# Gate and value products of the last two chunks by blocks of 128, group by group for both chunks

## The chip, the cores and the metric

One core of a Trainium2 chip runs the program. The metric is the device time of one execution in microseconds. The engines are TensorE (PE; its weight loads are shown as PEld), VectorE (DVE), ScalarE (ACT), GpSimd (POOL) and SyncE (SP, whose queue issues nearly all DMAs). All arithmetic is float32.

## The reference

An attention block with a threshold feeds a gated feed-forward block. What matters for the change is the second one.

```python
# q, k, v: (8, 8, 576, 64)
thresh = max(scores) - tau           # scores below thresh are dropped
x = softmax of what is left @ v      # -> (4608 tokens, 512)
g = x @ w_gate                       # (512, 1536)
val = x @ w_val                      # (512, 1536)
out = (g * sigmoid(g) * val) @ w_out # (1536, 512)
```

## The kernel before, in words

**Chunks.** The 4608 tokens are handled in nine chunks of 512. Chunks 0 to 7 are the first 512 tokens of each of the eight batches; the 64 tokens left over in each batch make up the ninth chunk, number 8. While the scores and the attention of batch b run, the feed-forward work of the batch before runs between them. Behind the last scores there is nothing left to run beside: the products of chunks 7 and 8 stand alone. This part, from the line `tail[0] = True` (L2321) on, is called the tail here.

**Groups.** Gate and value columns are taken in six groups (`NF2`) of 256 columns each. A group is a product of a token block (two halves of 256 tokens, by two halves of the 512 inputs) with a weight block (value and gate columns, by the same two halves). It is done as seven products of 256 x 256 x 256 in place of eight, with sums of the operands ahead of them and sums of the results behind them. The seven are the methods `p1` to `p7` of `Group` (L1092), done in the order p1, p4 of the group before, p5, p2, p6, p3, p7 (`gates_and_values`, L2157). Each `mul` (L1104) is four matmuls of 128 x 256. Results add up in PSUM: p1 fills a bank `a`, ACT copies it to a bank `b`, p2 adds to `a`, and p6, p7 and p4 add to `b` one after the other; between them ACT reads what `b` holds so far, multiplied by 0.5. `finish` (L1159) makes the gate: tanh on ACT, (1 + tanh) x value on DVE, times the gate half on POOL, or on DVE in the tail.

**Products by blocks.** In the tail `NestedGroup` (L1282) does two of the seven products, p5 and p3, by blocks of 128 once more: seven matmuls of 128 x 128 per block product in place of eight, which needs sums of blocks of x (`deepen_x`, L1258, on DVE) and of the weights (made long before, and read with the group's other weights from `sums_hbm`). Their results lie in two banks as seven blocks and are folded to a 256 x 256 result, by `fold` (L1218) from SBUF or by `fold_banks` (L1228) from PSUM.

**Weights.** A group has nine parts of 256 KB in `sums_hbm`. From chunk 2 on `load_flow` (L1034) reads them, for each chunk anew, in two DMAs of 1280 and 1024 KB into one of two places, two groups ahead.

**Outputs.** The six groups of a chunk give the hidden values `hall`, and `Deep` (L1640) multiplies them by the summed `w_out`, again as seven products, five of them by blocks of 128 in the tail. `early` (L1665), `late` (L1672) and `inner_sums` (L1684) sum hidden values for it, on DVE in the tail. Its first product `p1` runs ahead of the last group's p4 (`gates_end`, L1808). In the tail the order is: groups of chunk 7, outputs of chunk 7, groups of chunk 8, outputs of chunk 8. The tokens of chunk 8 come back from `last_hbm`, and `token_sums` (L1057) makes their three sums.

**What sets the order.** The TensorE products are written out in program order. Everything for DVE, ACT, POOL and SP goes through `Plan` (L28): each job has a cost, a rank and its dependencies, and the plan decides with these, at the time of writing the program, in which order each engine's queue holds them. On the chip each queue is worked in that order, and an instruction that waits holds up all behind it in its queue.

**Banks.** PSUM has eight banks. In the tail all are free for gates and values (`more_banks`, L2325).

Of the kernel before, what the change touches and what calls it, by code (L numbers as in the profile page):

```python
# [10 lines left out]
F32 = mybir.dt.float32  # L11
# [133 lines left out]
def kernel(  # L145
# [90 lines left out]
    e_tail = whole[:, ZONE + KW:ZONE + KW + CW]  # L236
# [13 lines left out]
    sums_hbm = hbm.tile([NF2, P, GW], F32, name="sums_hbm")  # L250
    stream_hbm = hbm.tile([3, P, 3 * QW], F32, name="stream_hbm")
# [840 lines left out]
    class Group:  # L1092
# [66 lines left out]
        def finish(self, t, gb, gj, hold, mv):  # L1159
# [9 lines left out]
            tt, eng, took = (dve_tt, "DVE", 0.62) if tail[0] else (pool_tt, "POOL", 1.3)  # L1169
# [12 lines left out]
        def p7(self):  # L1182
# [4 lines left out]
            tt, eng, took = (dve_tt, "DVE", 0.62) if tail[0] else (pool_tt, "POOL", 1.3)  # L1187
# [14 lines left out]
    AT = {0: (0, 0), 1: (0, 1), 5: (0, 2), 2: (0, 3), 3: (1, 0), 4: (1, 1), 6: (1, 2)}  # L1202

    class Seven(Buf):
# [23 lines left out]
        def fold_banks(self, banks_, *deps):  # L1228

            y = self.place.rearrange("p (x q) -> p x q", q=P)  # L1230
            q0, q1 = (h.ap().rearrange("p (x q) -> p x q", q=P) for h in banks_)
            twice = lambda x: x.broadcast_to((P, 2, P))
            j = job("ACT", 0.28, lambda: nc.scalar.copy(y[:, 4:5], q0[:, 0:1]), *deps, rank=0)
            j = job("DVE", 0.42, dve_tt(y[:, 0:2], twice(y[:, 4:5]), q0[:, 1:3], ALU.add), j, rank=0)
            j = job("DVE", 0.42, dve_tt(y[:, 3:5], twice(y[:, 1:2]), q1[:, 1:3], ALU.add), j, rank=0)
            j = job("DVE", 0.29, dve_tt(y[:, 1], y[:, 3], q0[:, 3], ALU.add), j, rank=0)
            j = job("DVE", 0.42, dve_tt(y[:, 2:4], twice(y[:, 4:5]), q1[:, 0:2], ALU.add), j, rank=0)
            return j, self.place[:, 0:DM].rearrange("p (f n) -> p f n", n=TC)

# [14 lines left out]
    sevens = {False: (Seven(s_main), Seven(e_main)), True: (Seven(vall[:, 0:CW]), Seven(e_tail))}  # L1254
    flat_s = deque([Flat(sevens[False][0])])
    x_deep = {}

    def deepen_x(c, *deps):  # L1258

        if tail[0]:  # L1260
            if "t" not in x_deep:
                x_deep["t"] = [qkp.tile([P, S], F32, name=name) for name in ("qT", "kT")]
            q_, k_ = x_deep["t"]
            ts = q_[:, 0:2 * P], q_[:, 2 * P:4 * P], k_[:, 0:2 * P], k_[:, 2 * P:4 * P]
        else:
            ts = *(x_main[:, n * 2 * P:(n + 1) * 2 * P] for n in range(3)), tmp.rearrange("p a f n -> p (a f n)")[:, 4 * HW:4 * HW + 2 * P]
            deps = *deps, *s_bufs[0].jobs
# [14 lines left out]
    class NestedGroup(Group):  # L1282
# [20 lines left out]
        def p5(self):  # L1303
            self.take_b()
            self.es = [take("pe") for _ in range(2)]
            m = self.nested(0, True, *(d for h in self.es for d in h.deps))
            self.s, e = sevens[tail[0]]
            self.c5 = self.s.fill(self.es, m, 0)
            self.s5 = self.s.fold("DVE" if tail[0] or self.g not in FOLDS[0] else "POOL", 0 if tail[0] else 1, *self.c5)

        def p3(self):
            m = self.nested(1, False, *self.c5)
            e = sevens[tail[0]][1]
            u = self.u1_buf
            if tail[0]:
                old, e.jobs = e.jobs, []
                j, y = e.fold_banks(self.es, m, *old)
                for h, full in zip(self.es, (True, False)):
                    h.read_by(j)
                    h.done(full)  # L1320
                g1 = job("DVE", 0.62, lambda: nc.vector.scalar_tensor_tensor(out=u.ap, in0=y, scalar=0.5, in1=u.ap, op0=ALU.mult, op1=ALU.add),
                         j, self.u1, rank=0)
            else:
                js = e.fill(self.es, m, 0)
                for h, full in zip(self.es, (True, False)):
                    h.read_by(js[1 if full else 0])
                    h.done(full)
                j = e.fold("DVE" if self.g not in FOLDS[1] else "POOL", 0, *js)
                g1 = job("DVE", 0.62, dve_tt(u.ap, u.ap, e.ap, ALU.add), j, self.u1, rank=0)
            e.jobs = [g1]  # L1330
            self.finish(0, u, g1, self.a, self.m2)
# [306 lines left out]
    AHEAD = 3  # L1638

    class Deep:  # L1640


        def __init__(self, c, mark):
            self.c = c
            halves = [hall[:, t].rearrange("p g f n -> p (g f) n") for t in range(2)]
            self.a11, self.a12, self.a21, self.a22 = (halves[t][:, k * NF2:(k + 1) * NF2] for t in range(2) for k in range(2))
            self.in_tail = tail[0]
            self.s2, self.s3 = (flow[:, lo:lo + KW].rearrange("p (f n) -> p f n", n=TC) for lo in (GW, GW - KW))
            self.place = flow[:, 0:KW]
# [4 lines left out]
            if tail[0]:  # L1654
                self.steps = deque([self.p1, self.gates_end, self.p2, self.p7_alone, self.p5_flat, self.p6_alone, self.p3_flat, self.p4_alone])
                self.spaces = [pall[:, n * CW:(n + 1) * CW] for n in range(5)]
                if c == B:
                    self.steps = deque([self.p1, self.gates_end, self.p2, self.p7_alone, self.p5_end, self.p6_alone, self.p4_alone, self.p3_end])
# [6 lines left out]
        def early(self, mark):  # L1665
# [4 lines left out]
            self.inner_sums(6, self.s3, free_place if self.in_tail else middle, j3)  # L1670
# [8 lines left out]
        def sum(self, out, a, b, op, x, *deps, rank=2):  # L1679
            fs = slice(2 * x, 2 * x + 2)  # L1680
            tt, eng, took = (dve_tt, "DVE", 0.62) if tail[0] else (pool_tt, "POOL", 1.3)
# [708 lines left out]
```

## Time and profile before

| what | value |
|---|---|
| three runs | 1349.41 us median (1348.5 to 1352.29) |
| the profiled execution | 1349.87 us; its span 1348.0, so 1.87 around it |
| granted TensorE clock | 1.00 |
| PE busy | 1334.6 us, 99% |
| DVE, ACT, POOL busy | 1066.5, 895.7, 778.0 us |
| DMA | 202.11 MB, 150 GB/s over the span |
| last attention product ends | 1130.86 us from the start of the span |
| groups of chunk 7 | 1135.74 to 1204.58, and p4 from 1209.27 to 1211.00 |
| outputs of chunk 7 | from 1204.58, until 1240.11 |
| groups of chunk 8 | 1240.11 to 1308.95, and p4 from 1313.64 to 1315.37 |
| outputs of chunk 8 | from 1308.95, until 1344.50 |

The busy table gives for each engine the busy time, its share of the span and the number of instructions. A float32 product is recorded as two records of a matmul, so a plain product of four matmuls counts x8 and one of seven blocks x14. The chain of waits goes back from the last instruction: at each step to what released it, or to the instruction before on its engine. A stretch line gives the busy time of each engine in a window, the granted clock, the busy share of the DMA engines and what they moved. In a timeline the columns are start, duration, engine, line, operation, out<-in and shape; what stands in brackets is the engine's idle time ahead of it and what ended it. PSUM banks carry the names pa, pb, pe, px, py and sc there. The helper `dve_tt` records all DVE sums at L928, `pool_tt` all POOL sums at L925.

### The profile page before, as it was taken

How to read it: one execution, taken by the hardware profiler on the slowest of the kernel's cores; microseconds unless marked ns; L12 is line 12 of the kernel's file. 1: busy time of each engine (PE TensorE's matmuls, PEld its weight loads, DVE VectorE, ACT ScalarE, POOL GpSimd, SP SyncE). 2: the span in 40 equal slices, each digit the busy share in tenths (PEclk: the TensorE clock that was granted, in tenths of full speed). 3: DMA queues.
4: the chain of work that ended last, by engine and by line, in shares of the span. 5: the costliest groups of instructions: out<-in, count | busy, mean ns of one | idle time of the engine just before them, and what ended most of it. 6: DMA issues, size and time to landing. Idle time of an engine off the chain costs nothing.

```text
span 1348.0 us, 40299 instructions
## 1 busy us (share of the span) xinstructions
PE 1334.6 (99%) x15914; PEld 1118.9 (83%) x15914; DVE 1066.5 (79%) x2860; ACT 895.7 (66%) x2315; POOL 778.0 (58%) x870
## 2 busy tenths in 40 slices
PE   9999999999999999999999999999999999999998
PEld 7777777787888878888888888887888889999998
DVE  7888898888887777888788888888788876586686
ACT  6888777767756677787777777778677773330330
POOL 2677497565685659745994689566965594000000
PEclk9999999999999999999999999999999999999999
DMA  8753324356557543746264636562565518524621
GB/s 178 206 186 96 79 58 133 122 149 177 153 166 225 169 126 92 211 137 203 62 201 145 216 97 195 158 215 69 139 212 145 171 57 270 195 96 165 210 80 32
DMA packets 216140, 202.11 MB, mean 150 GB/s; under 512 B 166800, under 2 KB 184208, under 8 KB 205200
## 3 DMA queue, kind: packets, MB, share of 16 engines
q1 hardware_dynamic: 212032, 198.62, 50.0%
q8 instruction: 126, 2.06, 0.6%
q10 hardware_dynamic: 3920, 0.92, 0.3%
q14 instruction: 62, 0.51, 0.1%
HBM read 172.36 MB, written 27.13 MB: 148 GB/s over the span
## 4 chain that ended last, share of the span: by engine, by line
PE 93%; DVE 2%; DMA 2%; POOL 1%; ACT 1%; issue 1%; SPq 0%; ACTq 0%; DVEq 0%; POOLq 0%
PE pb L1109 19%; PE pa L1109 13%; PE px L1711 12%; PE sc L1989 10%; PE xa L2088 9%; PE pe L1109 6%; PE po L1416 6%; PE pe L1294 4%; PE py L1711 3%; PE pv L1341 2%; PE pg L1341 2%; PE sc L1294 2%; PE py L1720 2%; PE sc L483 1%; PE pv L600 1%; DMA wo<-in_moe_w_gate_dram 1%
## 5 line engine op out<-in xcount | busy, mean ns | idle before, releaser
L2037 DVE SCALAR_TENSOR_TENSOR pall<-sc,th,pall 128x288 f32<-128x288 f32 x504 | 244.3, 513 | 42.0 <-ACT pall L2035 22.6
L1109 PE MATMUL pb<-xall,big 128*128 128x256 f32 x1152 | 273.9, 381 | 0.0
L2035 ACT ACTIVATE pall<-sc,nm 128x288 f32<-128x288 f32 x504 | 232.8, 498 | 33.6 <-DVE pall L2037 33.5
L1109 PEld LDWEIGHTS pb<-xall,big 128*128 128x128 f32 x1152 | 214.9, 190 | 30.7 <-issue 2.7
L2066 DVE STREAM_TRANSPOSE pall<-pall 128x576 f32<-128x576 f32 x252 | 188.4, 764 | 23.6 <-ACT pall L2064 15.6
L2064 ACT ACTIVATE pall<-pall,ri 128x288 f32<-128x288 f32 x388 | 179.0, 527 | 28.4 <-DVE ri L2052 27.5
L1109 PE MATMUL pa<-xall,big 128*128 128x256 f32 x768 | 183.1, 381 | 0.0
L925 POOL TENSOR_TENSOR hall<-hall,tmp 128x512 f32<-128x512 f32 x80 | 102.2, 1280 | 106.5 <-DVE hall L1164 86.0
L1109 PEld LDWEIGHTS pa<-xall,big 128*128 128x128 f32 x768 | 143.2, 190 | 21.7 <-issue 2.5
L2010 DVE TENSOR_REDUCE mx<-sc 128x2 f32<-128x576 f32 x168 | 125.9, 750 | 43.4 <-PE sc L1989 42.8
L925 POOL TENSOR_TENSOR big<-big 128x128 f32<-128x128 f32 (+3 forms) x174 | 129.1, 750 | 44.1 <-ACT big L1216 22.3
L1989 PE MATMUL sc<-kT,qT 64*32 64x288 f32 (+1 forms) x5376 | 144.7, 345 | 1.0 <-DVE pall L2037 1.0
L1989 PEld LDWEIGHTS sc<-kT,qT 64*32 64x32 f32 x5376 | 95.1, 106 | 50.0 <-issue 9.3
L2088 PE MATMUL xa<-pall,vall 64*32 64x288 f32 x4032 | 128.8, 404 | 0.4 <-PE px L1711 0.4
L2088 PEld LDWEIGHTS xa<-pall,vall 64*32 64x32 f32 x4032 | 75.4, 107 | 46.1 <-issue 4.3
L2061 POOL TENSOR_SCALAR pall<-pall,ri 128x288 f32<-128x288 f32 x116 | 58.7, 518 | 71.8 <-DVE ri L2052 70.0
L1109 PE MATMUL pe<-xall,big 128*128 128x256 f32 x384 | 91.4, 381 | 0.0
L2046 ACT COPY sums<-sums 32x6 f32<-32x6 f32 x336 | 66.6, 198 | 30.2 <-DVE pall L2037 26.1
L1163 ACT ACTIVATE vall<-tmp 128x512 f32<-128x512 f32 x96 | 59.9, 627 | 36.8 <-POOL tmp L925 17.3
L1109 PEld LDWEIGHTS pe<-xall,big 128*128 128x128 f32 x384 | 72.4, 190 | 11.1 <-ACT pall L2064 1.1
L2012 DVE TENSOR_REDUCE mx<-sc 128x1 f32<-128x288 f32 x168 | 75.0, 446 | 0.0
L925 POOL TENSOR_TENSOR big<-hall 128x384 f32<-128x384 f32 (+2 forms) x69 | 65.2, 969 | 14.6 <-PE pa L1109 14.5
(290 smaller groups left out, 2629.5 us busy)
## 6 DMA issues: line engine op xcount, KB each, us to landing
big<-sums_hbm SPq DMA_DIRECT2D x42, 1280.0 KB, 6.7
big<-sums_hbm SPq DMA_DIRECT2D x42, 1024.0 KB, 6.9
vall<-in_v_dram SPq DMA_DIRECT2D x112, 144.0 KB, 3.6
sums_hbm<-big SPq DMA_DIRECT2D x36, 256.0 KB, 3.6
out_dram<-big SPq DMA_DIRECT2D x32, 256.0 KB, 3.0
qT<-in_q_dram SPq DMA_DIRECT2D x112, 72.0 KB, 4.0
kT<-in_k_dram SPq DMA_DIRECT2D x112, 72.0 KB, 3.1
wo<-in_moe_w_gate_dram SPq DMA_DIRECT2D x16, 384.0 KB, 3.7
```

The costliest lines, as they stand in the source:

```text
L925: return lambda: nc.gpsimd.tensor_tensor(out=out, in0=a, in1=b, op=op)
L1109: nc.tensor.matmul(ps[:, i], w[:, k_, i * P:(i + 1) * P], x[:, k_, :], start=first and i == k_ == 0, stop=True, skip_group_check=True)
L1294: nc.tensor.matmul(self.es[b_].ap()[:, at_ * P:(at_ + 1) * P], ws[n], xd[o][n], start=b_ not in begun, stop=True, skip_group_check=True)
L1416: nc.tensor.matmul(ps, h(f), w[:, f, :], start=(f == 0), stop=(f == NF2 - 1))
L1711: nc.tensor.matmul(ps, a[:, f, :], ws[n][:, f, :], start=bank_ not in begun, stop=True, skip_group_check=True)
L1989: nc.tensor.matmul(pss[h][(slice(g * G, (g + 1) * G), *part)], qT[hs, col:col + G], kT[hs, c * SH + keys[0]:c * SH + keys[1]], start=True, ...
L2010: rs.append(job("DVE", 0.72, lambda n=n, tile_=tile_: nc.vector.tensor_reduce(out=mx[:, n:n + 2, 0], in_=tile_[:, :, 0:SH], axis=AX.X, op= ...
L2035: ej = job("ACT", 0.42, lambda x=x, n=n: nc.scalar.activation(ps[x], scs[x], AF.Exp, bias=nm[:, n:n + 1]), ej, masks.get((h, u - 1)), rank=0)
L2037: masks[x] = job("DVE", 0.45, lambda x=x, n=n: nc.vector.scalar_tensor_tensor(out=ps[x], in0=scs[x], scalar=th[:, n:n + 1], in1=ps[x], op0 ...
L2064: scaled.append(job("ACT", 0.46, lambda x=x, n=n: nc.scalar.activation(x, x, AF.Copy, scale=ri[:, n:n + 1]), rj, rank=rank))
L2066: seg["turned"].append(job("DVE", 0.72, lambda both=both: nc.vector.transpose(out=both, in_=both), *scaled, rank=rank))
L2088: nc.tensor.matmul(holds[a].ap()[x * G:(x + 1) * G, 0:SH].rearrange("d (i q) -> d i q", q=G), vr[rs, h, j, ds], p[rs, h, :, j, :], start=( ...
```

## The change

**Order.** In the tail the groups of the two last chunks stand side by side: group 0 of chunk 7, group 0 of chunk 8, group 1 of chunk 7, and so on, then the outputs of chunk 7, then those of chunk 8. A group is now a `Whole`, with the same seven products in the same order as before, all seven by blocks of 128.

**Banks.** The eight banks are four pairs; `a`, `b` and `e` are a pair each. All copies between them and all reads move 512 and 384 columns in two instructions. Results p2 and p4 are folded from PSUM into a stage in SBUF (`folded`), and the multiplication by 1 + tanh reads that stage. p3 is added to half of p6's sum on DVE and folded by POOL; p7 is added to p5 on DVE and folded there. The last multiplication of the gate, and `Deep`'s sums of chunk 7 ahead of its outputs, go to POOL.

**Weights.** Ten places of 512 columns hold one product's weights each, 256 KB read and 256 KB made from it. A place is loaded for the product ten places on when chunk 8's product has used it, and used by both chunks. Five of the seven products need four sums of 128 x 128 for it, made on POOL, one of the five on DVE (for the first ten places, three on DVE and two on POOL); the other two read ready sums with a second DMA.

**Tokens.** All seven token operands are summed by blocks (`deepen_all`), for chunk 7 on DVE and POOL after the last attention product, for chunk 8 during the first two groups. Chunk 8's tokens are loaded earlier, into another place.

**Gated values of chunk 8** are stored to `hall_hbm`, two DMAs of 256 KB per group, and read back in four DMAs of 768 KB during the outputs of chunk 7. In the last outputs p7 comes ahead of p2.

**Around it.** Some ranks change: the four sums that fold an output of chunk 6 come ahead of others on DVE, and sums for chunk 6's outputs go up by one rank on POOL. `NestedGroup` keeps only the part that is used before the tail.

```diff
+    CELL, NCELL, FIRST_CELL = 2 * HW, 10, 1
+    J = 0, 2, 1, 3, 5, 6, 4
+    SUM_ENG = {0: "POOL", 1: "DVE", 3: "POOL", 6: "POOL", 4: "POOL"}, {0: "DVE", 1: "DVE", 3: "DVE", 6: "POOL", 4: "POOL"}
...
+    def load_cell(N, *deps):
...
+        g, n = N // NQ, J[N % NQ]
+        place = cell(N)
...
+        base = job("SP", 0.5, lambda: nc.sync.dma_start(out=place[:, 0:HW], in_=sums_hbm[g][:, (n + 1) * HW:(n + 2) * HW]),
+                   *deps, lag=1.6, moves=0.9)
+        if n in (2, 5):
+            more = sums_hbm[g][:, 0:HW] if n == 2 else sums_hbm[g][:, (NS_ - 1) * HW:]
+            cell_loads[N] = base, job("SP", 0.5, lambda: nc.sync.dma_start(out=place[:, HW:], in_=more), *deps, lag=1.6, moves=0.9)
+            return
...
+        jt = job(eng, took, tt(t1, a21, a22, ALU.add), base, *deps, rank=rank)
+        jt = job(eng, took, tt(t2, t1, a11, ALU.subtract), jt, rank=rank)
+        jt = job(eng, took, tt(t4, a12, t2, ALU.subtract), jt, rank=rank)
+        cell_loads[N] = job(eng, took, tt(t3, a11, a21, ALU.subtract), jt, rank=rank), base
...
-    deepen_x(B - 1, plan.t + plan.PIPE)
+    deepen_all(B - 1, "DVE", -1, 0, 1, 1, fourths[0][:, 0:1], *deps, attended)
+    deepen_all(B - 1, "DVE", -1, 2, 2, 2, fourths[0][:, 1:3], *deps, attended)
+    deepen_all(B - 1, "DVE", 0, 5, 2, 1, fourths[1][:, 0:2], *deps, attended)
+    deepen_all(B - 1, "POOL", 1, 1, 2, 2, fourths[1][:, 2:4], *deps, attended)
...
-    for c in (B - 1, B):
-        for _ in gates_and_values(c):
-            pass
-        begin_outputs(c)
-        out_steps(2)
...
+        def product(self, n, both, first, *deps):
...
+                for x in ORDER:
+                    b_, at_ = AT[x]
+                    nc.tensor.matmul(both.ap(b_)[:, at_ * P:(at_ + 1) * P], ws[x], xd[x], start=b_ not in begun, stop=True,
+                                     skip_group_check=True)
...
+            m = pe(NEST, fn, *deps, *cell_loads[N], x_ready[self.c, X_OF[n]])
+            if self.c == B:
+                load_cell(N + NCELL, m)
...
+        def folded(self, both, m):
...
+            j = job("ACT", 0.28, lambda: nc.scalar.copy(y[:, 4:5], q0[:, 0:1]), m, *st.jobs, rank=0)
+            j = job("DVE", 0.42, dve_tt(y[:, 0:2], twice(y[:, 4:5]), q0[:, 1:3], ALU.add), j, rank=0)
...
+        def finish(self, t, u, gj, st, fj):
...
+            vj = job("DVE", 0.62, lambda: nc.vector.scalar_tensor_tensor(out=o, in0=n.ap, scalar=1.0, in1=o, op0=ALU.add, op1=ALU.mult),
+                     tj, fj, rank=0)
...
+        def p3(self):
+            m = self.product(5, self.e, False, *self.c5)
...
+            j = self.u.fold(GATE_FOLDS[self.c][0], 0, *js)
+            self.finish(0, self.u, j, self.st, self.fa)
+
+        def p7(self):
+            m = self.product(6, self.b, False, *self.u1)
+            self.u, _ = u2s[0], u2s.rotate(-1)
+            self.u2 = self.u.fill(self.b.holds, m, 0)
...
+    for g in range(NF2):
+        for c in (B - 1, B):
+            new = Whole(c, g)
+            new.p1()
+            if old is not None:
+                old.p4()
...
+            for fn in (new.p5, new.p2, new.p6, new.p3, new.p7):
+                fn()
...
+    begin_outputs(B - 1)
```

## The prediction

> **What bounds the kernel now.** First the page's busy table, then its chain of waits in order of time for the last 110 us, which is where the change lies.
>
> ```profile
> PE 1334.6 (99%) x15914; PEld 1118.9 (83%) x15914; DVE 1066.5 (79%) x2860; ACT 895.7 (66%) x2315; POOL 778.0 (58%) x870
> ...
> 1243.40 1.73 PE pa L1109 x8
> 1245.13 1.73 PE pb L1109 x8
> 1246.86 1.56 PE sc L1294 x14
> ...
> 1308.95 4.69 PE px L1711 x42
> 1313.64 1.73 PE pb L1109 x8
> ```
>
> TensorE works without a hole, and in the tail the chain is nothing but its products, so time goes only as TensorE's work or as waits put into it. A plain product (8 records) takes 1.73 us, one by blocks of 128 (14 records) 1.56. The products by blocks also run back to back inside px (42 records in 4.69, again 1.56 for 14), so a long row of them has no cost of its own in weight loads.
>
> Next the table of stretches: a stage with scores, the first gate stage of the tail, the second.
>
> ```profile
> 560.00:704.00 144.00, 144.00 (x2012) 120.91 (x2012) 118.03 (x339) 108.41 (x294) 102.64 (x117) 1.00 0.54 156
> 1136.00:1204.00 68.00, 68.00 (x398) 62.10 (x397) 45.10 (x91) 24.11 (x46) 0.00 (x0) 1.00 0.54 185
> 1240.00:1308.00 68.00, 68.00 (x399) 62.11 (x398) 45.73 (x92) 23.50 (x45) 0.00 (x0) 1.00 0.47 160
> ```
>
> Columns: length, then PE, PEld, DVE, ACT, POOL busy, clock, DMA. POOL does nothing in the tail, DVE is busy for 66%, and the clock is 1.00. Here the change spends.
>
> Last, the timeline in a stage where POOL works:
>
> ```profile
> 589.14 1.30 POOL L925 TENSOR_TENSOR tmp<-tmp,big 128x512 f32<-128x512 f32 x1 [2.26 <-ACT tmp L1186]
> ...
> 589.86 0.86 DVE L928 TENSOR_TENSOR big<-big 128x256 f32<-128x256 f32 x1
> ...
> 608.46 1.20 DVE L928 TENSOR_TENSOR tmp<-tmp,big 128x512 f32<-128x512 f32 x1
> ...
> 609.18 1.61 POOL L925 TENSOR_TENSOR tmp<-tmp,big 128x512 f32<-128x512 f32 x1
> ...
> 610.35 0.69 DVE L1164 SCALAR_TENSOR_TENSOR hall<-vall,pa 128x512 f32<-128x512 f32 x1
> ```
>
> The 128x256 sum takes 0.42 us in the tail; here 0.86, ending 0.28 after the POOL sum that was running. The 128x512 one takes 0.69 in the tail, here 1.20, and the POOL sum behind it 1.61 in place of 1.28. The sum at 610.35, with one operand in PSUM, keeps its 0.69 beside POOL. So a DVE sum with both operands in SBUF and a POOL sum exclude each other. I call those DVE sums **port sums**.
>
> **The change part by part.**
>
> *TensorE.* Per group and chunk five plain products become products by blocks. Six groups take 70.6 us now (1240.11 to 1308.95, and the 1.73 of the last p4). 42 products at 1.5625 (a third of 4.69) are 65.6. Two chunks: 2 x (70.57 - 65.63) = **-9.9 us**. The output products keep their number and kind. A group of one chunk will take 10.94.
>
> *ACT per group.* Four moves of a pair of banks, 512 and 384 wide (0.57 to 0.60 and 0.48 to 0.49, 1.08 together), two 128 copies (0.27), two tanh (0.63): 6.1 of 10.94. The tightest loop is p6, its copy, p7: one product, 1.56 us, lies between. ACT began 0.26 after the product in the old loop (product until 1142.33, ACT at 1142.59), needs 1.05, and TensorE starts 0.10 after a releaser (transposition until 1126.03, attend at 1126.13): 1.41. It fits by 0.15, so I cost it at nothing; a tanh in its way would cost up to 0.5.
>
> *DVE per group.* From PSUM: two folds of banks (3 x 0.42 + 0.29 = 1.54 each) and the half-scaled adds (0.69 + 0.55): 4.33. Port sums: the 896-wide add 1.08, a fold 1.54, two multiplications by 1 + tanh, which now read SBUF twice (0.69 each), and one weight in five, used for two chunks (2 x 0.29): 4.58 in nine. Together 8.91, or 81% of 10.94.
>
> *POOL per group.* Four weights in five, 16 sums of 128x128 per two chunks (8 x 0.46), a fold (3 x 0.73 + 0.46) and two gate multiplications (1.28 each), which stood on DVE: 8.88, also 81%.
>
> *The port.* No row shows this mix. Low end: no waits. High end: nine port sums meet POOL at random; POOL is in a sum 81% of the time, and what is left of it is 0.38 on the mean (sum of squares over twice the sum of its fourteen durations), so 0.31 per sum: DVE 11.70, 0.77 over TensorE, for twelve groups 9.2. The nearest row is the stage from 560 to 1126, where POOL is busy 72%: its 60 port sums are longer than alone by 0.10 on the mean (24 at 488 ns against 419, 12 at 857 against 686, 8 at 631 and 4 at 606 against 419, the other 12 not longer). By 0.81/0.72 that is 0.11 and DVE needs 9.9: TensorE stays the bound. I take 0.1 per group for a queue that slips: **+1.2** (0 to 9).
> The Trainium skill, SBUF — State Buffer, section "SBUF: two separate sides", calls the pair of ports that VectorE and GpSimd share an exclusive lock, held for the whole instruction, also for a VectorE instruction with two SBUF inputs, and the loser fully blocks. The rows above agree (0.86 for 0.42). The rule speaks against this change, which brings POOL back beside nine such sums; taken alone, with full exclusion, the two engines would need 8.88 + 4.58 = 13.5 us per group.
>
> *The start.* Now DVE is idle until 1128.93, does four sums of the last tile, four token sums from 1131.53 (ACT's copies end at 1131.59) and four x sums until 1134.68, and these are needed only at 1137.47. In the order of the changed kernel 15 weight sums (0.29 each) and the four of the tile (1.56) stand ahead of the token sums, then seven x sums (2.40), and the third block of the first product, at about 1135.9, waits for the second last of them. Without POOL: 1126.03 + 4.3 + 1.6 = 1131.9, + 1.7 + 2.4 = 1136.0: no stall. But POOL's 896-wide add (2.10, from 1126.79) and then nine sums of POOL share the port with these. Low end 0; high end the add's 2.1 and 0.31 for nine sums, 4.9. I take **+2.5**, half, since some weight sums get in ahead of the add. One weight sum stands before the last transposition that the last attend waits for, behind a load issued after 1121: **+0.5** (0 to 1). The sums for the last chunk (4.9 on DVE, 7.1 on POOL) come in the first two groups and are covered by the four pairs of banks: p3's pair is wanted again 3 us later, so DVE may be that late.
>
> *The DMA queue.* A group of the last chunk reloads nine parts of 256 KB and stores two: 2.9 MB in 10.94 us, 264 GB/s. The page's busiest slice moves 270, and 256 KB land in 3.0 to 4.4. But a place is refilled ten products (15.6 us) before its use, four sums (1.8) come between, and the group after loads nothing: nothing, and about 1 per group if POOL is so late that this cover is gone. SP's stores of the gates wait for POOL ahead of later loads; same cover.
>
> *The outputs.* The first chunk's sums go to POOL and before its outputs; those of the last come back by DMA during 35 us of outputs. p2's sums stand behind the last fold on DVE: **+0.5** (0 to 3). The end from 1344.5 is as before.
>
> **Sum**: -9.9 + 1.2 + 2.5 + 0.5 + 0.5 = -5.2. Against the profiled execution's own 1349.87 (span 1348.0 and 1.87 around it; 0.46 above the median of the runs, 1349.41): **1344.7**.
>
> **The rivals.**
> 1. *Nothing is lost.* For it: all three helpers stay under 82%, and now nothing waits. Against it: the start, where DVE has no slack even without POOL. 1349.87 - 9.9 = 1340.0.
> 2. *The port takes the gain.* Port sums wait 0.31, DVE needs 11.70 per group and sets the pace: +9.2, less 3 of lateness that the banks cover, + 3 at the start and for attend: -0.7, 1349.2. For it: DVE's chains of four dependent port sums meet POOL at each. Against it: the 0.10 measured.
> 3. *Slower: DVE and POOL hold each other.* Each waits for the other and both queues are in order, so a late one stops the other's next. Midway between 11.70 and the 13.46 of full exclusion is 12.6 per group: 12 x 1.64 = 19.7, less 3, + 3: +9.8, 1359.7. It decides from about 12.1 per group. For it: 81% on both engines. Against it: of each sum only a part excludes (0.28 of 0.42).
> That the products are not replaced is not among them: in the order as built TensorE has 240 fewer rows of 256 and 420 more of 128.
>
> **How the numbers follow.** Forecast (1341.5 to 1345.8) 0.38; rival 1 0.14; rival 2 (1345.8 to 1354) 0.30; rival 3 0.18. A measurement of this kernel tells about 0.3%, 4 us, from no change: faster 0.52, same 0.30, slower 0.18. The range 1340 to 1354 leaves out rival 3 and little else; its ends hold the bounds of the start and of the port.
>
> **What would show it.** Right: 10.94 us from group to group on TensorE with holes of tenths; a hole of some 2.5 us in the first product, released by DVE; 128x256 port sums of 0.45 to 0.55 on the mean. Wrong: port sums of 0.7 and more, groups of 11.5 and more with TensorE released by DVE or POOL (rival 2 or 3); holes released by a DMA of the weights; or no hole at the start.

## The result, and the profile after

| | median | runs |
|---|---|---|
| before | 1351.42 us | 5 (1348.5 to 1352.29) |
| after | 1372.81 us | 5 (1371.9 to 1373.89) |

The ratio is 1.0165, with a 95% interval from 1.0150 to 1.0179: the kernel is **slower by 1.65%**. The prediction of 1344.7 (1340 to 1354) was wrong in sign. The profiled execution took 1372.49 us, 22.6 more than that of before.

First the busy table and the chain of waits of the changed kernel.

```profile
PE 1334.8 (97%) x16274; PEld 1127.7 (82%) x16274; DVE 1124.5 (82%) x2930; ACT 908.9 (66%) x2363; POOL 918.1 (67%) x1048
...
PE 86%; DVE 5%; POOL 3%; DMA 2%; issue 2%; ACT 1%; SPq 0%; ACTq 0%; DVEq 0%; POOLq 0%
```

The chain of the kernel before:

```profile
PE 93%; DVE 2%; DMA 2%; POOL 1%; ACT 1%; issue 1%; SPq 0%; ACTq 0%; DVEq 0%; POOLq 0%
```

PE's share of the span fell from 99% to 97%, and in the chain DVE and POOL now hold 8% between them, 3% before. Next the table of stretches over the groups (length, then PE, PEld, DVE, ACT, POOL busy, clock, DMA share, GB/s): the start, a stretch in the middle, the end with the first outputs.

```profile
1136.00:1163.00 27.00, 21.41 (x175) 21.00 (x174) 25.99 (x53) 8.29 (x20) 15.68 (x20) 0.94 0.37 108
...
1230.00:1254.00 24.00, 22.58 (x199) 22.07 (x197) 21.13 (x39) 10.66 (x25) 20.47 (x29) 1.00 0.40 121
1254.00:1303.00 49.00, 39.08 (x334) 37.80 (x333) 45.54 (x67) 17.84 (x41) 41.47 (x43) 0.95 0.16 50
```

TensorE has holes (idle times) in all three, and where they are longest the clock is down as well. In the middle one pair of groups (one of each chunk) takes 24.0 us, from p1 to p1, in place of 2 x 10.94. There DVE and POOL are both busy for 85% and more; their busy time holds waits, as the following shows.

**One sum waits for another.** The timelines of DVE and of POOL in the same 2 us; then, from the groups of instructions between 1142 and 1296 us, two of DVE's (count, busy, mean ns, idle before), and one of POOL's from 1203.6 to 1251.7 us:

```profile
1128.20 2.19 DVE L928 TENSOR_TENSOR big<-big 128x128 f32<-128x128 f32 x1
...
1128.12 2.12 POOL L925 TENSOR_TENSOR tmp<-tmp 128x896 f32<-128x896 f32 x1 [0.45 <-ACT tmp L1753]
```

```profile
L928 DVE TENSOR_TENSOR tmp<-tmp 128x256 f32<-128x256 f32 x33 | 22.3, 676 | 0.8
...
L928 DVE TENSOR_TENSOR tmp<-tmp,pa 128x256 f32<-128x256 f32 x12 | 5.0, 417 | 0.3
```

```profile
L925 POOL TENSOR_TENSOR big<-big 128x128 f32<-128x128 f32 x34 | 19.2, 584 | 0.6
```

A DVE sum of 128x128, 0.29 us alone, took 2.19: it began 0.08 after a POOL sum and ended 0.15 after it. The folds from SBUF take 676 ns; the same shape with one operand in PSUM keeps its 417. Over the trace from 1127 to 1300 us, 155 of DVE's sums and multiplications have both operands in SBUF: 120 begin inside a POOL sum, which had 0.48 us to go on the mean, and these are 0.35 longer than alone; the other 35 are not longer at all. So what POOL has left is waited for, all but some 0.13 us. POOL waits too: its 128x128 sums take 0.58 us there on the mean, 0.46 alone.

**What stops TensorE.** In the middle stretch, TensorE, then ACT, then POOL:

```profile
1225.86 0.71 PE L2499 MATMUL pb<-xall,big 128*128 128x128 f32 x4 [1.07 <-ACT tmp L1249]
...
1224.15 0.63 ACT L2549 ACTIVATE kT<-big 128x512 f32<-128x512 f32 x1 [2.33 <-POOL big L925]
1224.68 0.25 ACT L2528 COPY pall<-pa 128x128 f32<-128x128 f32 x1
1224.83 0.49 ACT L1247 ACTIVATE tmp<-pb 128x384 f32<-128x384 f32 x1
1225.21 0.60 ACT L1249 ACTIVATE tmp<-pb 128x512 f32<-128x512 f32 x1
...
1216.62 7.96 POOL L925 TENSOR_TENSOR big<-big 128x128 f32<-128x128 f32 x12
```

TensorE waits for the fill that ends at 1225.81. p6, whose result it moves, had been done at 1223.2. The fill stood in ACT's queue behind a tanh that waited 2.33 us for POOL: there twelve sums in a row, weight sums and the gate's fold mixed, take 7.96 us, and the fold ends at 1224.11. From the eleventh cell on POOL's weight sums all belong to chunk 8's groups: 16 x 0.46 + 2.65 of fold + 2.56 of multiplications is 12.5 us alone, for a group of 10.94. So they run on into the next group of chunk 7, and there these lines stand.

**Start and outputs.** TensorE at both:

```profile
1137.22 0.61 PE L2499 MATMUL pa<-xall,big 128*128 128x128 f32 x4
1141.66 0.80 PE L2499 MATMUL pa<-qT,big 128*128 128x128 f32 x2 [3.83 <-DVE qT L928]
1142.25 0.75 PE L2499 MATMUL pa<-xall,big 128*128 128x128 f32 x2
...
1302.46 2.93 PE L1730 MATMUL px<-wo,hall 128*128 128x128 f32 x12 [6.01 <-ACT pall L1752]
```

The third block of the first product waits 3.83 us for DVE, as foretold but longer. Before the second product of the outputs it waits 6.01 us for ACT's copies, and the twelve records behind this hole take 2.93 in place of some 1.5. On ACT and DVE:

```profile
1299.36 0.63 ACT L2549 ACTIVATE kT<-big 128x512 f32<-128x512 f32 x1 [8.28 <-POOL big L925]
1301.31 0.63 ACT L2549 ACTIVATE vall<-tmp 128x512 f32<-128x512 f32 x1 [1.32 <-DVE tmp L928]
1301.84 0.57 ACT L1752 COPY pall<-px 128x512 f32<-128x512 f32 x1
...
1290.19 4.61 DVE L928 TENSOR_TENSOR big<-big 128x384 f32<-128x384 f32 x3
1294.72 0.68 DVE L2571 SCALAR_TENSOR_TENSOR big<-sc,big 128x512 f32<-128x512 f32 x1
```

The copies stand behind the last two tanh. The first waits for a fold on POOL, the second for one on DVE, and both folds begin late: DVE does three sums for the outputs ahead of the additions that they need. These sums take 0.55 us each alone and took 4.61 together beside POOL.

**The account**, from the starts of TensorE's records (by which a hole is 0.17 longer than the idle time in brackets), against the 22.6 us: products -9.9; the start 4.0; the groups from 1160 to 1287 us 15.0; the outputs 6.2; three stretches at half clock behind the holes of 4.0, 2.6 and 6.2 us, 1.5 each, 4.7; 1.3 that the profiled execution had lost before the changed part, and 0.4 ahead of the last attention. The sum is 21.7; the rest is gaps under 0.2.

### The profile page after: what moved, and what is told of

Its sections match the earlier page's. It is cut to its first block, busy times and chain, and to the rows that moved or that the text cites. A ratio compares the mean times of both kernels' runs of the same rounds, so it can differ in the third digit from the quotient of the medians.

```text
span 1370.7 us, 41554 instructions
## 1 busy us (share of the span) xinstructions
PE 1334.8 (97%) x16274; PEld 1127.7 (82%) x16274; DVE 1124.5 (82%) x2930; ACT 908.9 (66%) x2363; POOL 918.1 (67%) x1048
## 4 chain that ended last, share of the span: by engine, by line
PE 86%; DVE 5%; POOL 3%; DMA 2%; issue 2%; ACT 1%; SPq 0%; ACTq 0%; DVEq 0%; POOLq 0%
PE pb L1109 14%; PE px L1730 11%; PE sc L2020 10%; PE pa L1109 9%; PE xa L2119 9%; PE pe L1109 6%; PE po L1422 5%; PE py L1730 3%; PE pe L1309 3%; PE sc L2499 2%; PE pv L1347 2%; PE pg L1347 2%; POOL big L925 2%; PE py L1739 2%; PE pa L2499 2%
## 5 line engine op out<-in xcount | busy, mean ns | idle before, releaser
L2068 DVE SCALAR_TENSOR_TENSOR pall<-sc,th,pall 128x288 f32<-128x288 f32 x504 | 244.4, 514 | 41.3 <-ACT pall L2066 21.9
L925 POOL TENSOR_TENSOR big<-big 128x128 f32<-128x128 f32 (+3 forms) x284 | 196.7, 707 | 48.7 <-ACT big L1249 22.4
L2097 DVE STREAM_TRANSPOSE pall<-pall 128x576 f32<-128x576 f32 x252 | 188.4, 764 | 23.8 <-ACT pall L2095 15.6
L1109 PE MATMUL pb<-xall,big 128*128 128x256 f32 x864 | 205.8, 381 | 0.0
L1109 PEld LDWEIGHTS pb<-xall,big 128*128 128x128 f32 x864 | 161.2, 190 | 24.0 <-issue 2.7
L1109 PE MATMUL pa<-xall,big 128*128 128x256 f32 x576 | 137.7, 382 | 0.0
L1109 PEld LDWEIGHTS pa<-xall,big 128*128 128x128 f32 x576 | 107.8, 190 | 17.4 <-issue 2.5
L925 POOL TENSOR_TENSOR big<-hall 128x384 f32<-128x384 f32 (+2 forms) x72 | 69.7, 991 | 14.8 <-PE pa L1109 14.6
L925 POOL TENSOR_TENSOR hall<-hall 128x384 f32<-128x384 f32 (+2 forms) x70 | 71.4, 1035 | 0.8
```

Of the source, the lines that this page charges most:

```text
L925: return lambda: nc.gpsimd.tensor_tensor(out=out, in0=a, in1=b, op=op)
L1109: nc.tensor.matmul(ps[:, i], w[:, k_, i * P:(i + 1) * P], x[:, k_, :], start=first and i == k_ == 0, stop=True, skip_group_check=True)
L2068: masks[x] = job("DVE", 0.45, lambda x=x, n=n: nc.vector.scalar_tensor_tensor(out=ps[x], in0=scs[x], scalar=th[:, n:n + 1], in1=ps[x], op0 ...
L2097: seg["turned"].append(job("DVE", 0.72, lambda both=both: nc.vector.transpose(out=both, in_=both), *scaled, rank=rank))
```

## The experiments

The texts use the theories **A**: the port (DVE and POOL exclude each other; in its strict form, the sums at the port are what fills a pair of groups); **B**: POOL's crowding in chunk 8's groups, port or no port; **C**: late transfers or TensorE's own order; **D**: wrong costs in the plan; **E**: the order in ACT's queue. All times are medians; the kernel before ran beside them at 1348.9 to 1349.9, and at 1351.4 beside the changed kernel, so a difference from that kernel's 1372.8 may be up to 2.5 us too large; where this matters, the ratios to the kernel before are given. Six of the kernels leave out weight sums or put fills in their place: they tell a price, they are no versions.

### What the weight sums cost

Without those from the eleventh cell on:

```diff
+        if N >= NCELL:
+            cell_loads[N] = base,
+            return
         jt = job(eng, took, tt(t1, a21, a22, ALU.add), base, *deps, rank=rank)
```

> From the eleventh cell of the ring on, the four sums that make a cell's second half are left out (the products read what an earlier cell left there), so POOL loses about 16 sums of 0.46 us and more in each group of chunk 8; loads, products, folds and queues stay. Theory A (POOL's and DVE's sums hold each other at the shared port, and what is late stands in ACT's in-order queue): a pair of groups falls from 24.0 to 22.0-22.6 us, DVE's port sums keep 0.10 to 0.15 us of lengthening out of 0.28, and the whole takes 1354 to 1363 us. Theory B (the sums of the weights crowd POOL in chunk 8's groups, port or no port): the pair falls just as far, DVE's port sums keep what the folds and mults alone cause. Theory C (the ring's transfers come late, or the plan's order on TensorE itself is at fault): within 2 us of the changed kernel, 1372.8. Under A and B the hole of 4 us at the start stays, since the first ten cells are made as before.

**1360.2 us**. A pair of groups takes 21.9 (p1 at 1186.11, 1208.00, 1229.88), TensorE without a hole there. C is out: loads and TensorE's order are unchanged, and in the changed kernel DVE, not a load, ends POOL's idle times between 1203.6 and 1251.7 us. The holes at the start (4.0) and at the outputs (5.3) stay. Without any weight sums:

```diff
+        cell_loads[N] = base,
+        return
```

> The sums that make a cell's second half are left out for all cells, the first ten too (the products read what stood there before); loads, folds and queues stay. In the run without the sums from the eleventh cell on, the hole of 4.0 us in the first product stayed, and the whole took 1360.2 us. If that hole is DVE's time in the first ten cells' sums (about 15 sums before 1137 us, with their waits for POOL some 7 us of DVE), it shrinks to under 1 us, the clock stays up behind it, and the whole takes 1352 to 1356 us. If it is the chain from the last attention to the first activations' sums, the hole stays at 3 to 4 us and the whole at 1358 to 1361.

**1354.8 us**, with no hole in the first product: 5.4 us for the first ten cells, on DVE ahead of the token sums, as the first case said. The stretch table in its groups:

```profile
1190.00:1250.00 60.00, 60.00 (x540) 60.00 (x539) 46.57 (x93) 29.73 (x65) 34.67 (x35) 1.00 0.41 124
```

TensorE works 60.00 of 60 us: the products by blocks bring what was computed for them, once nothing holds them up.

### Port or crowding

Fills in place of the sums from the eleventh cell on, all of them on POOL:

```diff
+        if N >= NCELL:
+            fill_ = lambda: nc.gpsimd.memset(place[:, HW:HW + 432], 0.01)
+            jt = base
+            for _ in range(4):
+                jt = job("POOL", took, fill_, jt, *deps, rank=rank)
```

> From the eleventh cell on each of the four sums that make a cell's second half is replaced by a fill of 432 columns on POOL, meant to take about the same 0.46 us without reading SBUF (the second halves then hold a constant, so the weights are not the reference's). POOL's queue, its order and its planned load stay those of the changed kernel. Theory A (the shared port): DVE's port sums and POOL's folds fall back towards their own length, a pair of groups takes 22.0 to 22.8 us, the whole 1354 to 1364. Theory B (POOL's crowding by the clock, port or no port): the pair stays at 23.5 to 24.0 and the whole at 1368 to 1373, whatever the port sums do. If fills hold DVE too, both give about 1370 and the run tells nothing.

**1365.7 us**, between A's total and B's; a pair takes 22.4, though POOL now has more to do than in the changed kernel: 20 fills and 12 sums a pair, 19.6 us alone, against 28 sums of 17.8. But this kernel also takes four sums from DVE. So once more with POOL's sums alone replaced, DVE's kept (`if N >= NCELL and eng == "POOL"`):

> The changed kernel with each of POOL's weight sums from the eleventh cell on replaced by a fill of 432 columns, which took 0.456 us against 0.459 for the sum alone; DVE's weight sums, all queues, their order and the planned times stay as they are (these second halves then hold a constant). So only one thing differs from the changed kernel: these 16 instructions in each pair of groups do not read SBUF. In the earlier run with fills all five products' sums were fills, and DVE had four sums less; it gave a pair of 22.4 us. Theory A (port): the pair falls from 24.0 to 22.2-22.8 us and the whole to 1362-1367 us. Theory B (POOL's time and the order behind it): 23.5 to 24.0 and 1369-1373.

**1365.5 us**, a pair 22.4 to 23.1. POOL's fills in this run, and DVE's folds beside them; the last line is the same group in the changed kernel, over the same two pairs:

```profile
L1233 POOL MEMSET big<- 128x432 f32 x32 | 14.0, 456 | 0.6
```

```profile
L928 DVE TENSOR_TENSOR tmp<-tmp 128x256 f32<-128x256 f32 x12 | 7.0, 581 | 0.3
```

```profile
L928 DVE TENSOR_TENSOR tmp<-tmp 128x256 f32<-128x256 f32 x12 | 8.2, 682 | 0.3
```

A fill takes the 0.456 us of a sum and does not read SBUF. That alone brings 7.3 us of the 12.6 that the sums cost (by the ratios 0.46 of 0.82%): A for about half. The total lies in A's range, the pairs at or just above its 22.2 to 22.8. The other 5.3 go with POOL's time, with what stands behind it, and with DVE's four sums; these were not told apart. In the run with 20 fills a pair, from 1127 to 1290 us, 36 of DVE's sums began inside a fill and were 0.04 longer than alone; 68 began inside a POOL sum and were 0.46 longer. The Trainium skill, SBUF — State Buffer, section "Who interferes with whom", says that a VectorE instruction with two SBUF inputs contends with a GpSimd instruction that reads SBUF, not with one that only writes it: these numbers agree.

### One fold from POOL to DVE

```diff
-    GATE_FOLDS = {B - 1: ("POOL", "DVE"), B: ("POOL", "DVE")}
+    GATE_FOLDS = {B - 1: ("POOL", "DVE"), B: ("DVE", "DVE")}
```

> The changed kernel with the first gate fold of chunk 8's groups on DVE instead of POOL: four sums move, 2.7 us of POOL against 1.5 us of DVE alone; nothing is left out. Theory B (POOL is crowded in chunk 8's groups, and that is all): POOL's work there falls from 12.5 to 9.8 us, a pair of groups from 24.0 to 22-22.6 us, the whole to 1360-1366. Theory A (a DVE sum that finds POOL in a sum waits for its end, 0.35 us each time): DVE gets 4 sums more that wait, 10.4 us of work and some 3 of waits in such a group, and the pair stays at 23.5 to 25.5 us, the whole at 1370 to 1382.

**1363.2 us**, 9.6 less, the best that leaves nothing out; still 1.0103 (1.0086 to 1.0120) of the kernel before. A's forecast is refuted: DVE takes four sums more that wait, and yet the pair falls to 23.3. B's total is met, its pair (22 to 22.6) is not. The hole at the outputs is 0.9, but in the last pair TensorE now waits 3.7 us for a fill, where two sums for the outputs stand in DVE's queue among the sums of a fold. What is left in a pair, on TensorE and ACT:

```profile
1222.53 0.71 PE L2499 MATMUL pb<-xall,big 128*128 128x128 f32 x4 [1.01 <-ACT tmp L1249]
...
1220.81 0.63 ACT L2549 ACTIVATE vall<-tmp 128x512 f32<-128x512 f32 x1 [2.96 <-DVE tmp L928]
1221.35 0.25 ACT L2528 COPY pall<-pa 128x128 f32<-128x128 f32 x1
1221.49 0.49 ACT L1247 ACTIVATE tmp<-pb 128x384 f32<-128x384 f32 x1
```

Again a fill, of a product done at 1219.96, behind a tanh that waits for a fold. With this edit and no weight sums at all:

> No weight sums in any cell (left out; the products read what stood in the second halves), and the first gate fold of chunk 8's groups on DVE. What is left of the change is its products by blocks, its moves and its queues. Without the weight sums alone it took 1354.8 us, with a hole of 5.3 us and a clock at half behind it before the outputs; the fold on DVE alone left 0.9 of that hole. If the two causes add, the whole takes 1346 to 1350 us, level with the kernel before or just below; if DVE becomes the bound with four sums more, 1353 to 1358.

**1349.8 us**, ratio 0.9997 (0.9987 to 1.0007): level with before. By the ratios the two causes add within the noise: 1.26% for the weight sums, 0.62% for the fold, and 1.68% for both. Of the gain of 9.9 little is left over even so: TensorE still waits 7.1 us in five holes of 0.5 to 2.2 us, at the start and at the end of the groups, and some 1.7 in gaps under 0.2. In the profiled executions its work from the last attention on takes 216.9 us, 218.0 in the kernel before.

### Orders of the queues

Weight sums give way to other sums on POOL:

```diff
-        rank = 3 if N < NCELL else 0
+        rank = 3 if N < NCELL else 2
```

> One number changed: the weight sums from the eleventh cell on give way to folds and mults that are ready (rank 2 for 0), all else computed as in the changed kernel. Theory B (crowding and order on POOL): the gate fold of chunk 8 no longer stands behind weight sums, the holes of 0.5 and 1.2 us in each pair shrink to under 0.5 in all, the whole takes 1360 to 1367 us. Theory A (the port): the sums stay as long as they are, folds gain their place but DVE and POOL meet as often; a pair falls by at most 0.8 us, the whole takes 1367 to 1372. Theory C: no change, 1371 to 1374.

**1374.0 us**. The pair falls only to 23.8, and at the end TensorE waits 10.4 us for POOL's sums of the last cells, pushed back until they were late. A's and B's totals were missed; C's is met by its number alone, for the holes have moved and no load ends one. The plan told the measured durations:

```diff
+            longer = slow.get(eng, 0.0)
+            took, less = took + longer, less + longer
...
+    slow.update(DVE=0.28, POOL=0.14)
```

> The plan of the tail is told longer sums, as the trace of the changed kernel shows them: DVE's sums with both operands in SBUF 0.28 us longer, POOL's 0.14. Nothing else is edited; only the order in the engines' queues can move. Theory D (the work fits, the queues are in the wrong order since the plan believes in shorter sums): the holes before fills of u2 go, also the 6.2 us before the outputs, and the whole takes 1355 to 1365 us. Theory A (port, work held up whatever its order): 1368 to 1376 us. Theory B: 1365 to 1372, since only the order against the weight sums can help.

**1395.4 us**: TensorE waits 3 to 5 us once or twice in each pair, for fills. All theories missed it. Both tanh behind the fills (the gate's fold counts as ready 5 us later), with the fold on POOL and on DVE:

```diff
-            return job(eng, took, tt(y[:, 4:6], twice(6), y[:, 4:6], ALU.add), j, rank=rank)
+            return job(eng, took, tt(y[:, 4:6], twice(6), y[:, 4:6], ALU.add), j, rank=rank, lag=5.0 if "late" in late else 0.0)
...
+    late.add("late")
```

> The changed kernel with one thing in the plan: a gate's folded sum counts as ready for tanh 5 us later than before, so that in ACT's queue both tanh of a group stand behind the fills of that group, which TensorE waits for. The sums, their engines and their number stay; nothing is left out. Theory E (the port makes the sums late, but what turns that into TensorE's holes is the order in ACT's queue: a fill that is ready stands behind a tanh that waits for a late fold): the holes released by ACT's fills go, a pair of groups falls from 24.0 to 22.0-22.6 us, the whole takes 1360 to 1366 us; the 4.0 us at the start stay. Theory A in its strict form (the port's sums, 26.9 us in a pair, are what is full, whatever the queues): the pair stays at 23.4 to 24.0 and the whole at 1369 to 1376. A tanh that is later may also hold buffers and make the outputs late: then holes appear in other places and the whole takes over 1376.

> The same edit of the plan, and the first gate fold of chunk 8's groups on DVE, as in the run that took 1363.2 us with 1.2 us of hole in each pair of groups; nothing is left out. Theory E: that hole goes (its fill had been ready 0.1 us before TensorE wanted it and stood behind a tanh), a pair takes 21.9 to 22.2 us, the whole 1355 to 1360 us. Theory A in its strict form (25.8 us of sums at the port in a pair): the pair stays at 23.0 to 23.4 and the whole at 1361 to 1366.

**1401.5 and 1388.7 us**. E as I stated it falls, by the way named last in the first expectation; in the second run E's total and A's were both missed. TensorE, ACT and POOL of the first of the two:

```profile
1231.44 0.71 PE L2501 MATMUL sc<-pall,big 128*128 128x128 f32 x4 [4.12 <-ACT tmp L1249]
...
1230.41 0.49 ACT L1247 ACTIVATE tmp<-sc 128x384 f32<-128x384 f32 x1 [2.06 <-POOL hall L925]
...
1229.12 1.26 POOL L925 TENSOR_TENSOR hall<-pall,tmp 128x512 f32<-128x512 f32 x1
```

No tanh is ahead of this fill. It waits for its place: p7's result has one place (`u2s`), and the gate's last multiplication frees it. A later tanh means a later multiplication, so fill, fold, tanh, multiplication, fill is a loop, and it leaves no room to put tanh last.

### Moving sums

The sums for the sixth product of the outputs behind the groups, alone, and with no weight sums (the edit shown there):

```diff
-                if (c, g) == (B, NF2 - 1) and fn == new.p6:
-                    state["deep"].sixth_sums(plan.t + plan.PIPE)
...
+            if self.c == B - 1:
+                self.sixth_sums(plan.t + plan.PIPE)
```

> The changed kernel with one call moved: the four sums for the sixth product of chunk 7's outputs are issued behind the last product of the groups instead of behind the fourth product of the last group. Nothing is left out. Theory A (three of these sums of 0.55 us take 1.5 each on DVE, since each waits until POOL's sum of 1.3 us ends, and stand ahead of the last multiply-add of a gate, so tanh is late and the copies of the outputs' first product stand behind it): the hole of 6.2 us before the second outputs' product falls to 1 to 3 us, the clock does not halve behind it, and the whole takes 1366 to 1370 us, unless the sixth product then waits. If the hole comes from the folds and tanh alone: 1372 to 1374.

> Both edits together: no weight sums in any cell (left out) and the sixth product's sums behind the groups. What then remains of the change is its products by blocks, folds, moves and queues. If the weight sums at the shared port and the crowding at the outputs are what turned the gain, it comes out below the kernel before: 1342 to 1350 us (60 products of 0.17 us less are 10 us, less some 3 to 5 us of short waits). If something else holds the tail (transfers, the order on TensorE, banks), it stays at 1354 to 1360.

**1374.5 and 1355.3 us**. The idle time at the outputs falls from 6.0 to 1.9 us, and the sixth product then waits 2.6 for the sums moved: the work on DVE is late, not one order of it. The second run lies in the other case of its expectation, that something else holds the tail. Weight sums by one instruction for two cells that lie side by side in the ring (128x2x128), alone, and with the fold on DVE:

```diff
+        mate = {1: N + 1, 3: N - 1, 6: N + 1, 4: N - 1}.get(n)
...
+        y = cells[:, lo:lo + len(Ns) * CELL].rearrange("p (c q) -> p c q", c=len(Ns))
+        a11, a21, a12, a22, t2, t3, t4, t1 = (y[:, :, x * P:(x + 1) * P] for x in range(8))
```

> Nothing is left out. The weight sums of the products 1 and 3, and of 6 and 4, whose cells lie side by side in the ring, are made by one instruction for both (128x2x128 instead of twice 128x128), 1 and 3 on DVE, 6 and 4 on POOL; at the start the sums of the cells 2 and 3 come behind the first activations' sums, and those of cell 7 behind the first product. Counted from durations alone, in a pair of groups the sums that need the port fall from 17.8 us on POOL and 9.1 on DVE (26.9 in all) to about 15.1 and 9.7 (24.8). Theory A (the port is what is full: 26.9 gave 24.0 us a pair, 25.8 with the fold on DVE gave 23.3, 18.5 without weight sums 21.9): a pair takes 22.5 to 23.0 us, the hole at the start falls to under 2 us, and the whole takes 1356 to 1363 us. Theory B (POOL's crowding alone): POOL falls by 2.7 us as with the fold on DVE, so a pair of 23.3 and 1360-1364. Both are near each other here; the next run tells them apart.

> The run before with the first gate fold of chunk 8's groups on DVE as well; nothing is left out. The port's sums: POOL 12.5 us, DVE 11.2, 23.7 in all in a pair of groups. Theory A: a pair takes 21.9 to 22.4 us, short waits are left, and the whole takes 1350 to 1356 us, level with the kernel before or a little slower; at the end the hole of 6.2 us stays under 1 as with the fold on DVE alone. If DVE is now what holds the groups (8.7 us with PSUM operands, 11.2 at the port, and its waits: over 21.9), the pair stays at 23 and the whole at 1358 to 1364.

**1376.7 and 1387.2 us**, above all that was expected, with holes of 2.4 to 3.6 and of 4.2 to 5.0 us in every pair. Less work at the port and slower: the strict form of A is refuted. I had counted durations, not what a queue holds up. POOL's and ACT's timeline in the first:

```profile
1240.17 2.54 POOL L925 TENSOR_TENSOR big<-big 128x256 f32<-128x256 f32 x3 [4.70 <-DMA big<-sums_hbm]
1242.67 1.26 POOL L925 TENSOR_TENSOR hall<-big,tmp 128x512 f32<-128x512 f32 x1
...
1243.96 0.49 ACT L1260 ACTIVATE tmp<-sc 128x384 f32<-128x384 f32 x1 [1.14 <-POOL hall L925]
```

A sum for two cells waits for the second cell's load, 4.70 us, and behind it in the queue stands the multiplication that frees the place. Last, the fold on DVE and the sums of cells 2, 3, 7 and 9 taken out of the start:

```diff
+        if N in (2, 3, 7, 9):
+            later_sums[N] = sums
...
+    for N in (2, 3):
+        later_sums[N](x_ready[B - 1, 4], rank=0)
```

> Nothing is left out. The first gate fold of chunk 8's groups on DVE (alone: 1363.2 us), and of the first ten cells' sums only those of cell 0 stand ahead of the first activations' sums on DVE; those of cells 2 and 3 come behind them, those of 7 and 9 behind the first product of chunk 8. In the run with sums in pairs the hole at the start stayed at 4.0 us since the pair's sums, moved in the text, were still ahead of the activations' sums in DVE's queue. If the hole is DVE's queue, it falls from 4.0 us to under 0.5, the clock no longer halves behind it (1.5 us), and the whole takes 1356.5 to 1359; if it is something else there (a transfer, POOL's share of the activations' sums), it stays over 2.5 us and the whole at 1361 to 1364.

**1366.1 us**, above both cases. The first hole falls to 0.91 and 0.58: it was DVE's queue. But the moved sums are then late themselves:

```profile
1137.86 0.49 PE L2506 MATMUL pa<-qT,big 128*128 128x128 f32 x2 [0.91 <-DVE qT L928]
1138.92 0.49 PE L2506 MATMUL pa<-xall,big 128*128 128x128 f32 x2 [0.58 <-DVE xall L928]
1144.77 0.49 PE L2506 MATMUL pa<-xall,big 128*128 128x128 f32 x2 [2.20 <-DVE big L928]
```

## Why the prediction was wrong, by its steps

- **TensorE, -9.9**: right. 10.94 us a group is what the run without weight sums shows.
- **The port, "that is 0.11 ... I take 0.1 per group for a queue that slips: +1.2"**: this step failed first. The mean of 0.10 came from a stage in which only 16 of 60 port sums begin inside a POOL sum; those 16 were 0.39 longer. I scaled it by POOL's busy share (0.81 over 0.72) and not by how often a port sum meets POOL: in the changed groups 120 of 155 do, so 0.27. My own high end, 0.31 from random meetings, was near. With 0.27 for nine sums DVE needs 11.3 us a group (8.91 + 2.4), 0.4 over TensorE; measured were 12.0, and the next two steps have the rest. Measured for the groups in all: 15.0, and 1.5 of clock.
- **ACT, "it fits by 0.15 ... a tanh in its way would cost up to 0.5"**: failed second. I priced the tanh's own length. A tanh at the head of the queue costs what it waits for, 2.33 us in the lines above, of which 1.24 reached TensorE.
- **POOL per group, 8.88**: an average over two unlike groups. Chunk 8's hold all its weight sums and need 12.5 us in 10.94.
- **The start, +2.5 (0 to 4.9)**: the cause was right (5.4 us without these sums), the size was not: 4.0, and 1.5 of half clock behind it, which the sum did not have. The +0.5 for the last attention was about right (0.4).
- **The outputs, +0.5 (0 to 3)**: failed, 6.2 and 1.5. I looked at p2's sums behind the last fold. What came late were the last two folds, behind three output sums on DVE, with the copies of the outputs' first product behind their tanh.
- **The DMA queue, nothing**: right, no hole of the changed kernel is released by a load.
- **Rivals**: the third had the mechanism (each waits for the other, queues in order), with 12.6 us a group and 19.7 in all where 12.0 and 16.5 were measured; it missed the outputs and the clock. It was given 0.18, since I held the measured 0.10 to be the nearest row. The sentence on the Trainium skill that spoke against the change had the direction right: its 13.5 us a group was 1.5 too high, my 11.04 was 1.0 too low.

What stays open: why the plan with the measured costs comes out that much worse was seen only as far as its holes (fills that wait for their place). A second place for p7's result was not tried. Of the versions that leave nothing out none came below the kernel before.

## What to carry to other kernels

A mean wait from another stage is worth nothing until it is split by whether the two instructions met; count in the new stage how many will. An engine's load is to be checked per period of the work that sets the pace, not averaged over unlike groups, and a wait at the head of an in-order queue is priced by what it waits for. Where a helper's result returns into the loop through a single place, reordering queues only moves the hole.

## What the runs showed of the hardware

**Half clock behind a hole.** In these traces the stretches at half clock begin on a grid of 3.41 us, each trace with an offset of its own, and last one or more of its steps: those at 1141.54, 1179.09 and 1298.56 us in the changed kernel lie 11 and 35 steps apart. What decides is how long TensorE idles within one step. Over all the traces from 1100 us on, taking steps at full clock, none of 1145 with under 1.8 us of idle time was followed by half clock, all 53 with over 1.95 were, and 3 of the 14 between.

So the length of a hole alone does not tell. The hole at 1286 us, 2.1 long, left the clock at 1.00 in the changed kernel (1.6 us of it in one step) and halved it where the sixth product's sums were moved (1.9); one of 3.4 that fell on two steps cost nothing (1.7 in the fuller), and all of 3.5 and more cost the clock. The three stretches in the changed kernel cost about 1.5 us each. The Trainium skill, TensorE: Matmul & The Clock Gate, section "Part 1: The HAM clock gate (the "warmup" mystery)", gives an idle window of about 3.4 us that runs freely. The grid agrees; that the whole window be idle was not needed here.

**The wait is not the whole rest.** A port sum that finds POOL in a sum ends 0.13 us sooner than the rest of that sum and its own length would make it (0.35 longer, with 0.48 to go).
